# Moving the state sums of even chunks from GpSimd to VectorE, and one weighting of queries from VectorE to GpSimd

## The chip, the cores and the metric

The kernel runs on one core of one Trainium2 chip. The metric is the device time of one execution in microseconds. Engine names in the profile: PE is TensorE (PEld its weight loads), DVE is VectorE, ACT is ScalarE, POOL is GpSimd, SP is SyncE, which here only issues DMAs.

## The reference, cut to what matters

A gated linear attention over 4 batches, 8 heads, 768 positions and a head size of 48 feeds a mixture of eight experts. The change touches only the attention:

```python
state = zeros((B, H, D, D)); y = zeros_like(q)
for t in range(S):
    state = alpha[:, :, t, :, None] * state + einsum('bhd,bhe->bhde', k[:, :, t], v[:, :, t])
    y[:, :, t] = einsum('bhd,bhde->bhe', q[:, :, t], state)
```

The experts' part (a gate with argmax, `relu(x @ w1[e]) @ w2[e]` for each token's expert, times its gate) takes the last two thirds of the time and is the same in both kernels.

## The kernel before, in words

The 768 positions are cut into chunks of 128, 6 for each batch, so 24 chunks in all (`i` is 0 to 23; `i % 6` is the place within its batch). Even and odd chunk make a pair `p`. The loop at line 1060 goes over `UNITS`: rounds 0 and 1 take chunks 0 and 1 singly, rounds 2 to 11 the pairs (2,3) to (20,21), rounds 12 and 13 chunks 22 and 23 singly. All five queues are in manual order there: each engine runs its instructions in the order in which the Python program issues them.

Each round `n` works on three units at once:

- VectorE prepares unit `n`. `decay` (line 346) runs a backward scan over the decay factors (L349), takes the chunk's whole decay into `amin` (L352) and weights the keys (L357 to L359). `decay_back` (line 362) runs a scan forward (L365, L366) and weights the queries (L367). The scan L349 needs the pairwise products `pp` of `products` (L325), and L367 needs queries that `queries` (L332) has multiplied by alpha in place; GpSimd does both for a later pair, except that in round 2 VectorE does `queries` for its own pair (2,3).
- TensorE takes unit `n-1` through `natural` (transposes of the keys, L378, which ScalarE copies out as `knat`, L380), `update` (the key-value product of each chunk, L454), `scores` (L390; ScalarE copies them out, L394, GpSimd masks them, L395) and `state` (L416, queries times the carried state `T1`). `update` is not run for the last chunk of a batch.
- Units `n-2` (`outputs`, L428) and `n-3` (`rows`, L472, and `logits`, L491, every other round) follow.

In `update`, ScalarE copies the product from PSUM to the SBUF tile `S1` (L456), and GpSimd adds the carried state (L459, left out for the first chunk of a batch) and multiplies by the decay, which gives the state for the next chunk, `T1[(i + 1) % 4]` (L461). So `state` of chunk `i` needs the L461 of chunk `i - 1`; for the odd chunk of a pair that is the even chunk of the same unit, in the same round.

The order on TensorE in a round is: `natural` and `rows` (and `logits`), then `update`, `outputs(n-2)`, `scores` of the even chunk, `scores` of the odd chunk, `state`.

PSUM has eight banks. Two hold the decay factors `GF`, two the tile `y`, and the other four are one ring, in which `natural`, `rows`, `logits`, `update` and `scores` take the next place in turn (line 89: the names `tr`, `rt`, `lg` and `sc` are all `(lps, "tr", 4)`). A place is free again when the last reader of its old tile is done. `update` takes one place, and `scores` two for each chunk (line 385), so the second tile of the odd chunk's scores is the fourth tile after `update`'s and takes its place. Within `scores` the two tiles of a chunk are written by turns.

The program closes the loop's pools after round 13 and goes on with the experts, whose first weights and rows come by DMAs that the routing on VectorE sets off in rounds 12 and 13.

Of the kernel before, what the change touches and what calls it, by code (L numbers as in the profile page):

```python
# [16 lines left out]
ALU = mybir.AluOpType  # L17
# [7 lines left out]
B, H, S, D = 4, 8, 768, 48  # L25
# [48 lines left out]
def attention_moe(ctx: ExitStack, tc: tile.TileContext, q, k, v, alpha, mid, wg, mb, w1, w2, turned, rowsv, small, out):  # L74
    nc = tc.nc
    vec, act, pool, pe, sp = nc.vector, nc.scalar, nc.gpsimd, nc.tensor, nc.sync
# [41 lines left out]
    def turns(shape):  # L118
        return ring_tile("lg", shape)
# [13 lines left out]
    PP = [na.tile([W, 2 * NP * SG + 1], F32, name=f"pp{i}") for i in range(2)]  # L133
# [40 lines left out]
    def load_part(p, z, c0=0, c1=2):  # L174
        t = TAP[p % NA2] if z == 2 else TKP[z][p % NB]
        return sp.dma_start(t[:, c0 * KW : c1 * KW], turned[p, :, z * K2 + c0 * KW : z * K2 + c1 * KW])
# [46 lines left out]
    GF = GT[:, : 2 * NP * SG]  # L223
# [15 lines left out]
    T1 = []  # L239
# [76 lines left out]
    def span(u):  # L316
        return u[0] // 2, u[0] % 2 * NP, (u[-1] % 2 + 1) * NP

    def pairs(t, a, b):
        return t.rearrange("w (s m e) -> w s m e", m=HP, e=2)[:, a:b]  # L320
# [8 lines left out]
    def queries(u, by):  # L329
        p, a, b = span(u)  # L330
        x = pairs(TK[1][p % NB], a, b)
        by.tensor_tensor(x[:, :, :, 0], x[:, :, :, 0], pairs(TA[p % NA2], a, b)[:, :, :, 0], op=ALU.mult)  # L332

    def scaled(u, name):
        n = len(u)
        t = (na if n == 2 else sb).tile([W, n, NP, P], F32, name=f"{name}{n}", bufs=2)
        for c, i in enumerate(u):
            st[i, name] = t[:, c]
        return pairs(t.rearrange("w c a t -> w (c a t)"), 0, n * NP)

    def factors(a, b):
        f = GF.rearrange("w (s m) -> w s m", m=SG)[:, a:b, :HP].unsqueeze(3)
        f = f.broadcast_to([W, b - a, HP, 2])
        return bass.AP(f.tensor, f.offset, [*list(f.ap)[:-1], [1, 2]])
# [17 lines left out]
    def decay_back(u):  # L362
        p, a, b = span(u)
        x, y = a * SG, b * SG
        vec.reciprocal(GF[:, x:y:SG], GF[:, x:y:SG])  # L365
        scan = vec.tensor_tensor_scan(GF[:, x:y], PP[p % 2][:, x:y], GF[:, x:y], 0.0, op0=ALU.mult, op1=ALU.max)  # L366
        vec.tensor_tensor(scaled(u, "q"), pairs(TK[1][p % NB], a, b), factors(a, b), op=ALU.mult)  # L367
        return scan

    def guard(p):  # L370
        act.activation(
# [26 lines left out]
    def tiles4():  # L398
        for h in range(2):
            for g in range(2):  # L400
                for c in range(2):
                    yield 2 * h + c, h, g, slice(64 * c, 64 * c + 64)

    def place_of(i, g, h):
        return slice((i % 2 * 2 + h) * P, (i % 2 * 2 + h + 1) * P)

    def state(u):
        y = ps.tile([P, 2, 4 * P], F32, name="y")
        st[u, "new"] = {(g, c): True for g in range(2) for c in range(2)}
        for i in u:  # L410
            st[i, "Y"] = y
            if i % NC == 0:
                continue
            for j, h, g, z in tiles4():
                r = slice(64 * g, min(64 * g + 64, W))
                pe.matmul(  # L416
                    y[z, g, place_of(i, g, h)],
                    T1[i % 4][r, j],
                    st[i, "q"][r, j],
                    start=st[u, "new"].pop((g, j % 2), False),  # L420
                    stop=False,
                )

    def outputs(u):
# [17 lines left out]
        for i in u:  # L442
            st[i, "yt"] = yt

    def update(u):
        u = [i for i in u if i % NC < NC - 1]
        if not u:
            return
        kv = turns([W, len(u), NP, D])
        for c, i in enumerate(u):  # L450
            kn, vt = st[i, "n"], VT[i % NV]
            for h in range(H):
                r = slice(64 * (h % 2), min(64 * (h % 2) + 64, W))
                pe.matmul(kv[r, c, h // 2], kn[:, h // 2, r], vt[:, h * D : (h + 1) * D], start=True, stop=True)  # L454
        S1 = na.tile([W, 2, NP, D], F32, name="S", bufs=2)
        act.copy(S1[:, : len(u)], kv)  # L456
        for c, i in enumerate(u):
            if i % NC > 0:
                pool.tensor_tensor(S1[:, c], S1[:, c], T1[i % 4][:, :, :D], op=ALU.add)  # L459
            A = amin[:, i + 1].unsqueeze(2).broadcast_to([W, NP, D])  # L460
            pool.tensor_tensor(T1[(i + 1) % 4][:, :, :D], S1[:, c], A, op=ALU.mult)  # L461

    def rows(u):
        if u[0] < NF:
# [586 lines left out]
    def unit(n):  # L1051
        return UNITS[n] if 0 <= n < NN else ()
# [7 lines left out]
    for n, u in enumerate(UNITS):  # L1060
        p = u[0] // 2
        ahead = u[0] % 2 == 0
        if n == 0:
            load_part(2, 2)
        if n == 4:
            sp.dma_start(xd[MID : MID + 1], zr)
            sp.dma_start(gd[MID : MID + 1], zr[:, 0:1])
        if n == 0:
            products(u, vec)
            queries(u, pool)  # L1070
            products((1,), pool)
        if ahead and p + 1 < NPR and n > 3:
            products((2 * p + 2, 2 * p + 3), pool)
        scan = decay(u)
        if n == 2:
            queries(u, vec)
        last = u[-1] % 2 == 1
        done = [i for i in unit(n - 3) if i % LB == LB - 1]
        turned_now = [i for i in unit(n - 1) if i % NC < NC - 1]
        if not done:  # L1080
            for i in turned_now:
                natural(i)
        if n == 2:
            guard(0)
        if ahead and n and p + 2 < NPR:
            behind(load_part(p + 2, 2), scan)
        if last and p + 2 < NPR:
            load_part(p + 2, 0)
        if n <= 2:
            fill(2)  # L1090
        if unit(n - 3):
            rows(unit(n - 3))
        for i in done:
            logits(i, LB)
        if done:
            for i in turned_now:
                natural(i)
        for i in done:
            logits_rows(i, LB)
        spot()  # L1100
        if n == NN - 2:
            next(first_early)
        if n == NN - 1:
            for _ in first_early:
                pass
            run_later()
        scan = decay_back(u)
        if n == 0:
            queries((1,), pool)
        if ahead and n and p + 1 < NPR:  # L1110
            behind(load_rows(p + 1), scan)
        for i in done:
            if i == GROUPS[0][0]:
                logits_sum(i - LB, LB)
            if i >= GROUPS[0][0]:
                logits_sum(i, LB)
            groups(i)
            if i == GROUPS[1][0]:
                first_early = group_flow(*GROUPS[1][1:])
                next(first_early)  # L1120
                next(first_early)
            if i == GROUPS[2][0]:
                now["s"] += 1
                advance(2)
                second_half(st["chosen"])
        if last and p + 2 < NPR:
            load_part(p + 2, 1)
        if n == 6:
            vec.tensor_copy(prev_, rev)
        if n == 9:  # L1130
            half_index()
        if n == 1:
            bias = bias_table()
        update(unit(n - 1))
        if last and n > 2:
            guard(p)
        if n == 1:
            products((2 * p + 2, 2 * p + 3), pool)
        if n == NN - 2:
            next(first_early)  # L1140
            next(first_early)
        if unit(n - 3):
            rows_out(unit(n - 3))
        if unit(n - 2) and n != 2:
            outputs(unit(n - 2))
        for i in unit(n - 1):
            scores(i)
        if n == 2:
            outputs(unit(n - 2))
        if unit(n - 1):  # L1150
            state(unit(n - 1))
        if n in (2, 3):
            products((2 * p + 2, 2 * p + 3), pool)
        if last and 1 <= p and p + 1 < NPR and n > 1:
            queries((2 * p + 2, 2 * p + 3), pool)
        if n == 2:
            guard(p)
        if n == 1 or 4 <= n <= 6:
            next(bias, None)
        if 5 <= n <= 9:  # L1160
            next(consts, None)
        if n == 1:
            fill(2)
        spot()
        if NN - 3 <= n < NN - 1:
            next(first_early)
        if NN - 4 <= n < NN - 2:
            held_out((n - NN + 4) * NF // 2, NF // 2)
# [280 lines left out]
    op0 = layer2_sum(hs[0], w2s[0], 0, 2)  # L1449
# [6 lines left out]
    op1 = layer2_sum(hs[0], w2s[0], 1, 2)  # L1456
# [11 lines left out]
    for n in range(1, len(seq)):  # L1468
# [4 lines left out]
        x, w = n % NX, n % 2  # L1473
# [160 lines left out]
```

## Time and profile before

| what | value |
|---|---|
| time, median of 3 runs | 331.51 us (331.22 to 332.39) |
| time of the profiled execution | 332.0 us |
| its span, first to last instruction | 330.2 us |
| mean granted TensorE clock | 0.995 |
| busy in the span: PE, DVE, ACT, POOL | 315.9, 199.0, 190.2, 187.1 us |

The span is cut into 40 slices of 8.3 us on the profile's page; there TensorE stands at 9 tenths from the fourth to the last but one, VectorE in slices 2 to 9, and GpSimd in the fourth and in slices 6 to 10. The attention loop ends at about 106 us. The time of the profiled execution is 1.8 us more than its span.

### The profile page before, as it was taken

The numbers are of one execution on the slowest core, as the hardware profiler recorded it, in microseconds if no ns is written. First come the engines' busy times: TensorE is split into PE (matmuls) and PEld (weight loads), VectorE is DVE, ScalarE is ACT, GpSimd is POOL, SyncE is SP. The second block draws the span as 40 slices with busy tenths as digits, with TensorE's granted clock in tenths as the row PEclk, the third lists the DMA queues.
The fourth block names the chain that finished last, engine by engine and source line by source line (L and its number), as shares of the span: only waits on it lengthen the run. The fifth ranks groups of instructions, "written<-read, shape, count | busy, mean of one in ns | idle before, by whom it ended". The sixth has DMA issues, their size and how long they took to land.

```text
span 330.2 us, 8690 instructions
## 1 busy us (share of the span) xinstructions
PE 315.9 (96%) x3417; PEld 278.9 (84%) x3418; DVE 199.0 (60%) x380; ACT 190.2 (58%) x344; POOL 187.1 (57%) x259
## 2 busy tenths in 40 slices
PE   8889999999999999999999999999999999999992
PEld 3678888897987779999889988998899888888991
DVE  5999999997784668883671575157515660175200
ACT  3777878787866543565436743674367444664210
POOL 6779799999783540778886396239423801230121
PEclk9999999999999999999999999999999999999997
DMA  7988998999678497996586198419742673100011
GB/s 255 414 304 282 325 299 284 311 286 318 207 225 308 148 318 268 355 326 204 152 198 227 37 278 219 136 36 289 231 138 40 229 164 123 48 30 0 3 50 55
DMA packets 44038, 67.04 MB, mean 203 GB/s; under 512 B 15993, under 2 KB 30488, under 8 KB 43988
## 3 DMA queue, kind: packets, MB, share of 16 engines
q1 hardware_dynamic: 37652, 53.50, 51.9%
q0 software_dynamic: 4000, 9.68, 8.4%
q10 hardware_dynamic: 2336, 3.22, 2.7%
q8 instruction: 29, 0.48, 0.6%
q14 instruction: 21, 0.17, 0.2%
HBM read 53.79 MB, written 9.50 MB: 192 GB/s over the span
## 4 chain that ended last, share of the span: by engine, by line
PE 61%; POOL 15%; issue 12%; DVE 6%; DMA 3%; ACT 2%; POOLq 1%; ACTq 0%; DVEq 0%
PE sc L1331 8%; PE sc L1333 8%; PE sc L1332 8%; PE tr L1352 7%; PE tr L1351 7%; PE tr L1350 7%; POOL scT L395 4%; PE tr L165 3%; PE y L428 3%; POOL pp L325 3%; POOL tq L332 2%; PE tr L390 2%; PE tr L472 2%; POOL S L459 2%; POOL out_dram L1272 2%
## 5 line engine op out<-in xcount | busy, mean ns | idle before, releaser
L1272 POOL DMA_INDIRECT out_dram<-os,odx x23 | 23.5, 1021 | 84.7 <-ACT os L1365 78.4
L1331 PE MATMUL sc<-w2H,hH 128*128 128x384 f32 x192 | 64.8, 338 | 0.0
L1333 PE MATMUL sc<-w2H,hL 128*128 128x384 f32 x192 | 64.3, 335 | 0.0
L1332 PE MATMUL sc<-w2L,hH 128*128 128x384 f32 x192 | 64.2, 334 | 0.0
L1015 ACT ACTIVATE hH<-tr 128x512 fp32r<-128x512 f32 x47 | 28.1, 598 | 49.0 <-PE tr L1352 43.0
L1350 PE MATMUL tr<-xH,w1H 128*128 128x512 f32 (+1 forms) x144 | 53.9, 374 | 0.0
L1352 PE MATMUL tr<-xH,w1L 128*128 128x512 f32 (+1 forms) x144 | 53.5, 372 | 0.0
L1351 PE MATMUL tr<-xL,w1H 128*128 128x512 f32 (+1 forms) x144 | 53.5, 372 | 0.0
L1017 DVE SCALAR_TENSOR_TENSOR hL<-tr,hH 128x512 fp32r<-128x512 f32 x47 | 32.3, 689 | 29.8 <-ACT hH L1015 29.6
L885 POOL DMA_INDIRECT xg<-xd,idx x25 | 27.4, 1097 | 19.9 <-DVE vals L671 13.0
L1365 ACT ACTIVATE os<-sc,gg 128x384 f32<-128x384 f32 x23 | 13.4, 582 | 43.1 <-PE sc L1333 41.5
L1323 DVE TENSOR_TENSOR xL<-xg,xH 128x512 fp32r<-128x512 f32 x12 | 8.3, 692 | 48.5 <-ACT xH L1322 48.5
L1331 PEld LDWEIGHTS sc<-w2H,hH 128*128 128x128 f32 x192 | 36.0, 188 | 1.2 <-issue 1.0
L1332 PEld LDWEIGHTS sc<-w2L,hH 128*128 128x128 f32 x192 | 36.1, 188 | 0.2
L1333 PEld LDWEIGHTS sc<-w2H,hL 128*128 128x128 f32 x192 | 36.0, 188 | 0.1
L891 POOL DMA_INDIRECT gg<-gd,idx x25 | 27.3, 1092 | 11.0 <-issue 7.0
L395 POOL TENSOR_SCALAR_AFFINE_SELECT scT<-scT 128x512 f32<-128x512 f32 x48 | 28.9, 635 | 7.8 <-ACT scT L394 7.8
L1352 PEld LDWEIGHTS tr<-xH,w1L 128*128 128x128 f32 x144 | 27.1, 188 | 5.0 <-DVE w1L L1035 0.5
L1351 PEld LDWEIGHTS tr<-xL,w1H 128*128 128x128 f32 x144 | 27.1, 188 | 4.7
L1350 PEld LDWEIGHTS tr<-xH,w1H 128*128 128x128 f32 x144 | 27.1, 188 | 4.5
L1035 DVE TENSOR_TENSOR w1L<-w1r,w1H 128x768 fp32r<-128x768 f32 x24 | 23.0, 997 | 8.8 <-ACT w1H L1033 8.6
L1035 DVE TENSOR_TENSOR w2L<-w2r,w2H 128x768 fp32r<-128x768 f32 x24 | 26.4, 1100 | 0.7
(280 smaller groups left out, 608.0 us busy)
## 6 DMA issues: line engine op xcount, KB each, us to landing
w1r<-in_moe_w_dram SPq DMA_DIRECT2D x16, 768.0 KB, 7.8
w2r<-in_moe_w_dram SPq DMA_DIRECT2D x16, 768.0 KB, 6.5
ta<-in_turned_dram SPq DMA_DIRECT2D x11, 512.0 KB, 4.9
tk<-in_turned_dram SPq DMA_DIRECT2D x11, 512.0 KB, 5.1
tq<-in_turned_dram SPq DMA_DIRECT2D x11, 512.0 KB, 6.4
vt<-in_rowsv_dram SPq DMA_DIRECT2D x11, 384.0 KB, 4.7
xd<-xs ACTq DMA_DIRECT2D x7, 384.0 KB, 6.3
xd<-w2r SPq DMA_DIRECT2D x2, 768.0 KB
```

Of the source, the lines that this page charges most:

```text
L395: pool.affine_select(s, s, [[0, NP], [1, P]], ALU.is_ge, 0.0, base=0, channel_multiplier=-1)
L885: pool.indirect_dma_start(xg[x][:, u], None, xd[0:rows], IOA(idx[:, c : c + 1], 0), bounds_check=rows - 1, oob_is_err=False)
L1015: act.activation(hH, hp, AF.Relu)
L1017: vec.scalar_tensor_tensor(hL, hp, 0.0, hH.bitcast(F32), op0=ALU.max, op1=ALU.subtract)
L1035: vec.tensor_tensor(lw, src, hi.bitcast(F32), op=ALU.subtract)
L1272: return pool.indirect_dma_start(to, IOA(odx[:, c : c + 1], 0), t, None, bounds_check=N - 1, oob_is_err=False)
L1331: pe.matmul(op, hH[:, us] if f is None else hH[:, f, us], wH, start=first, stop=False)
L1332: pe.matmul(op, hH[:, us] if f is None else hH[:, f, us], wL, start=False, stop=False)
L1333: pe.matmul(op, hL[:, us] if f is None else hL[:, f, us], wH, start=False, stop=final)
L1350: pe.matmul(hp, wH[:, d, fs], XH[:, d, :n], start=(d == 0), stop=False)
L1351: pe.matmul(hp, wH[:, d, fs], XL[:, d, :n], start=False, stop=False)
L1352: pe.matmul(hp, wL[:, d, fs], XH[:, d, :n], start=False, stop=(d == ND - 1))
```

## The change

`queries` for pair (2,3) moves from VectorE in round 2 to GpSimd in round 1, behind that round's `state`. `decay_back` is split behind its scan: from round 4 on, `update` of unit `n-1` is called between the scan (L366) and the weighting of the queries (L367, now `decay_queries`), where it stood behind both and behind the routing work of the round before. In `update`, for units that begin with chunk 4 or a later even chunk, the even chunk's add and multiply go to VectorE, which adds in place in PSUM (`kv[:, 0]`) and writes `T1` from there; ScalarE copies only the odd chunk to `S1`, and nothing where the odd chunk ends a batch. The odd chunk's add and multiply stay on GpSimd.

```diff
     def decay_back(u):
         p, a, b = span(u)
         x, y = a * SG, b * SG
         vec.reciprocal(GF[:, x:y:SG], GF[:, x:y:SG])
-        scan = vec.tensor_tensor_scan(GF[:, x:y], PP[p % 2][:, x:y], GF[:, x:y], 0.0, op0=ALU.mult, op1=ALU.max)
+        return vec.tensor_tensor_scan(GF[:, x:y], PP[p % 2][:, x:y], GF[:, x:y], 0.0, op0=ALU.mult, op1=ALU.max)
+
+    def decay_queries(u):
+        p, a, b = span(u)
         vec.tensor_tensor(scaled(u, "q"), pairs(TK[1][p % NB], a, b), factors(a, b), op=ALU.mult)
-        return scan
...
+    BY_VEC = 4
+
     def update(u):
...
+        c0 = 1 if u[0] >= BY_VEC and u[0] % 2 == 0 else 0
         S1 = na.tile([W, 2, NP, D], F32, name="S", bufs=2)
-        act.copy(S1[:, : len(u)], kv)
+        if len(u) > c0:
+            act.copy(S1[:, c0 : len(u)], kv[:, c0:])
         for c, i in enumerate(u):
+            by, s = (vec, kv[:, c]) if c < c0 else (pool, S1[:, c])
             if i % NC > 0:
-                pool.tensor_tensor(S1[:, c], S1[:, c], T1[i % 4][:, :, :D], op=ALU.add)
+                by.tensor_tensor(s, s, T1[i % 4][:, :, :D], op=ALU.add)
             A = amin[:, i + 1].unsqueeze(2).broadcast_to([W, NP, D])
-            pool.tensor_tensor(T1[(i + 1) % 4][:, :, :D], S1[:, c], A, op=ALU.mult)
+            by.tensor_tensor(T1[(i + 1) % 4][:, :, :D], s, A, op=ALU.mult)
...
         scan = decay(u)
-        if n == 2:
-            queries(u, vec)
...
         scan = decay_back(u)
+        if n > 3:
+            update(unit(n - 1))
+        decay_queries(u)
...
-        update(unit(n - 1))
+        if n <= 3:
+            update(unit(n - 1))
...
             state(unit(n - 1))
+        if n == 1:
+            queries((2 * p + 2, 2 * p + 3), pool)
```

## Rows read from the trace of the kernel before

**Rows 1.** The page's first part: busy time, share of the span, instructions.

```profile
PE 315.9 (96%) x3417; PEld 278.9 (84%) x3418; DVE 199.0 (60%) x380; ACT 190.2 (58%) x344; POOL 187.1 (57%) x259
```

**Rows 2.** The chain that ended last: start us, us, what.

```profile
38.90 2.40 POOL scT L395 x4
...
77.56 0.52 POOL T L461
```

**Rows 3.** Busy time in one stretch: length, then each engine, clock, DMA.

```profile
58.00:78.00 20.00, 19.49 (x479) 17.62 (x474) 17.56 (x29) 16.82 (x33) 19.20 (x29) 1.00 0.92 294
```

**Rows 4.** Waits of PEld and of DVE, 24 to 106 us: total, times, longest.

```profile
PEld tr L454 <- ACT knat L380: 3.6, 10, 0.7
PEld y L416 <- POOL T L461: 1.1, 2, 0.7
...
DVE rk L601 <- ACT kept L115: 4.8, 2, 3.4
```

**Rows 5.** VectorE in order of time, rounds 2 to 4: start, us, what.

```profile
15.88 1.57 DVE L332 TENSOR_TENSOR tq<-tq,ta 112x512 f32<-112x512 f32 x1
...
20.20 1.25 DVE L349 TENSOR_TENSOR_SCAN GF<-pp,GF 112x520 f32<-112x520 f32 x1
...
26.53 1.25 DVE L349 TENSOR_TENSOR_SCAN GF<-pp,GF 112x520 f32<-112x520 f32 x1
...
30.19 1.25 DVE L366 TENSOR_TENSOR_SCAN GF<-pp,GF 112x520 f32<-112x520 f32 x1
```

**Rows 6.** GpSimd in order of time.

```profile
18.98 1.51 POOL L332 TENSOR_TENSOR tq<-tq,ta 112x512 f32<-112x512 f32 x1 [2.08 <-DMA tq<-in_turned_dram]
...
25.19 1.04 POOL L325 TENSOR_TENSOR pp<-ta 112x512 f32<-112x512 f32 x1
...
29.34 0.51 POOL L461 TENSOR_TENSOR T<-S,amin 112x192 f32<-112x192 f32 x1
...
43.96 1.04 POOL L325 TENSOR_TENSOR pp<-ta 112x512 f32<-112x512 f32 x1
```

**Rows 7.** The load of pair (2,3)'s queries on SP, and such loads' landing times.

```profile
6.58 0.48 SPq L176 DMA_DIRECT2D tq<-in_turned_dram  x1
...
DMA to landing us min/median/max: 4.7/6.1/7.4
```

**Rows 8.** TensorE in order of time.

```profile
27.34 1.98 PE L390 MATMUL tr<-q,k 48*64 48x128 f32 x64
29.14 1.42 PE L416 MATMUL y<-q,T 64*64 64x128 f32 x32
...
50.11 0.61 PE L454 MATMUL tr<-vt,knat 128*64 128x48 f32 x15 [0.50 <-ACT knat L380]
...
75.20 1.98 PE L390 MATMUL tr<-q,k 48*64 48x128 f32 x64
...
78.12 0.67 PE L416 MATMUL y<-q,T 64*64 64x128 f32 x16 [0.51 <-POOL T L461]
```

**Rows 9.** GpSimd's adds, and two VectorE operations of other sizes.

```profile
L459 POOL TENSOR_TENSOR S<-S,T 112x192 f32<-112x192 f32 x9 | 5.4, 595 | 0.3
...
L359 DVE TENSOR_TENSOR k<-tk,GF 112x512 f32<-112x512 f32 x8 | 5.5, 690 | 0.3
...
120.28 0.26 DVE L773 TENSOR_TENSOR nj<-kv,thr 128x96 f32<-128x96 f32 x1 [0.52 <-PE kv L772]
```

**Rows 10.** VectorE in order of time, the first scans of rounds 7 and 10.

```profile
46.12 1.25 DVE L349 TENSOR_TENSOR_SCAN GF<-pp,GF 112x520 f32<-112x520 f32 x1
...
69.46 1.23 DVE L349 TENSOR_TENSOR_SCAN GF<-pp,GF 112x520 f32<-112x520 f32 x1
```

**Rows 11.** The end: TensorE's last matmul, then busy time and clock by stretch.

```profile
323.37 0.34 PE L1333 MATMUL sc<-w2H,hL 128*128 128x384 f32 x1
...
326.00:327.00 1.00, 0.00 (x0) 0.00 (x0) 0.00 (x0) 0.00 (x0) 0.00 (x0) 0.87 0.57 201
327.00:328.00 1.00, 0.00 (x0) 0.00 (x0) 0.00 (x0) 0.00 (x0) 0.00 (x0) 0.50 0.07 20
```

## The prediction

> **What bounds the kernel now.** I read the page first. By busy time TensorE fills 96% of the span [rows 1], which says little of a stage, so I went to the chain of waits. From 38.9 to 78 us it runs almost only through GpSimd: masks, products, query weightings, state sums, one behind the other, until the state multiply that ends at 78.08 [rows 2]. A reader who stops there would say that GpSimd bounds the loop. But busy time by stretch shows TensorE busy for 19.49 of 20 us between 58 and 78, as much as GpSimd's 19.20, and VectorE at 17.56 [rows 3]. And TensorE's waits from round 4 to the loop's end show what GpSimd costs it: 1.1 us for the state multiply, in two places. The larger one, 3.6 us for `knat`, is a trip from TensorE to ScalarE and back, which the change leaves alone [rows 4]. So GpSimd's 39 us in the chain hide about 1 us of loss; TensorE's own work lies right below. I then read VectorE, GpSimd and TensorE in order of time, to place the moved instructions between their neighbours.
>
> **The change part by part.**
>
> *Queries of pair (2,3).* VectorE loses one instruction of 1.57 us at 15.88 [rows 5]; the next one follows some 1.5 us after its start, so round 2 ends, with a little lost between dependent operations, 1.3 us earlier, and the first scan of round 3 starts at 18.9 instead of 20.2 [rows 5]. GpSimd must do it in time. Its load is issued at 6.58 and lands within 7.4 us, by 14.0 at the latest [rows 7]; the weighting then runs to 15.5 at a price of 1.51 [rows 6]. That pushes round 2's work on GpSimd back by up to 2 us, but GpSimd stands for 2.08 us ahead of 18.98, waiting for the next pair's queries [rows 6], and this wait hides it; without it the 1.5 us would stay on GpSimd's queue. What is late next is the product for round 4's scan: it lies behind that same DMA on GpSimd and ends at 26.23 [rows 6]. VectorE, free by 25.1, waits for it, and round 4 starts at 26.3 instead of 26.53 [rows 5]. Of 1.3 us VectorE keeps 0.2; TensorE keeps more, since its scores in round 4 can start up to 1.2 us before their 27.34 [rows 8] (their queries come from round 3).
>
> *Price of a sum on VectorE.* No row has 192 elements with a source in PSUM. Below lies 0.26 us for 96 elements out of PSUM, above it 0.69 for 512 [rows 9]; on a line between them 192 elements take 0.36. GpSimd's 0.60 for the same add [rows 9] is the far end. I take 0.35, so 0.8 for an add and a multiply that depend on each other, and 0.4 for a multiply alone.
>
> *Where the sum stands.* This decides. In round 4 GpSimd did the multiply for chunk 4 at 29.34 to 29.85 [rows 6], and TensorE's `state` waited for it a little. Now it stands on VectorE behind round 4's forward scan. That scan starts 3.66 us after the round's first (30.19 less 26.53 [rows 5]), so at 29.96; it ends at 31.2, and add and multiply at 32.0: 2.2 us later than on GpSimd, though each is cheaper.
>
> *What waits for it.* `state` of chunk 5, and before it something that the diff doesn't name. The even chunk's product now stays in its PSUM place until VectorE's multiply is done; ScalarE's copy used to free it right behind the product. The ring has four places, and the fourth tile after it is the second one of chunk 5's scores. On TensorE round 4 then goes: scores of chunk 4 from 26.15 to 27.1 (half of the 1.8 us between 27.34 and 29.14 [rows 8]), a standstill to 32.0, scores of chunk 5 to 32.95, `state` to 33.95. Before, `state` ended at 29.14 + 1.42 = 30.56 [rows 8]. TensorE leaves round 4 later by 3.4 us. Queued behind are the rest of the loop and the experts; ScalarE's copies and GpSimd's masks of chunk 5's scores follow it.
>
> The standstill itself can have a price. The granted clock is 1.00 between 58 and 78 us [rows 3]. At the end TensorE's last matmul ends at 323.71; the clock averages 0.87 in the stretch 326 to 327 and 0.50 in the next [rows 11], so it fell from 2.4 to 1.2 GHz some 3 us after TensorE had stopped. A standstill of 4.9 us is longer than that; TensorE's longest wait from round 4 on was 0.7 [rows 4]. The Trainium skill (TensorE: Matmul & The Clock Gate, What's actually happening) calls the slow clock the resting state, which activity lifts; by that rule TensorE would come out of the standstill slow, and the trace's end agrees (0.50). I leave it out of the sum and take it as a rival.
>
> *Does it stay?* From round 5 on TensorE has its 3.4 us of lateness and hardly a wait to lose them in: only the one for GpSimd in round 10, 0.7 us on the weight loads [rows 4], 0.51 on the matmuls ahead of 78.12 [rows 8], goes, as GpSimd has less to do. VectorE is hardly late at first (its sum of 0.8 less the 0.2 that it gained), but then falls back. Round 7's product on GpSimd (43.96 [rows 6]) follows masks that are now 3.4 late, so its scan starts at 48.4 instead of 46.12 [rows 10]. In round 7 VectorE must wait for the key-value product (50.11 + 0.6 + 3.4 = 54.1 [rows 8]; its scan is done at 53.3), the new wait, with the queries' weighting and the routing behind it. With that 0.8 and 0.65, 0.3 and 0.65 us for rounds 7, 8 and 9 (0.8 or 0.4 of sums, less the short gap ahead of L367 that they fill), less one wait of 0.2, round 10 starts at 69.46 [rows 10] + 4.5 = 74.0. Its sum is done 5.7 us later (30.19 + 1.25 - 26.53 [rows 5], and 0.8), at 79.7. TensorE wants the ring's place at 75.20 + 3.4 + 0.95 = 79.55 [rows 8], so the two meet there at almost no cost. In round 10 `state` ends at 81.5 instead of 78.8: 2.7 us late. In rounds 12 and 13 VectorE had waited 4.8 us for ScalarE's copies of the routing counts [rows 4]; they cover its lateness, and the first expert's loads keep theirs within about 0.4 us of TensorE's. ScalarE's copies that go were off the path. The experts then start 2.7 us late and end so.
>
> **Sum.** 332.0 us for the profiled execution, + 3.4 - 0.7 = 334.7. It lies 0.5 above the median of 331.5, so I predict **334.2 us**.
>
> **The rivals.**
>
> *The place is not what stops TensorE; only `state` is.* If the second scores tile finds another place, chunk 5's scores finish by 28 and only its `state` waits until 32.05 and ends at 32.6: 2.0 later, less the 0.7, so 1.3 and 332.8. For it: the trace of before shows no wait on this place. Against it: the names of the ring all lead to one pool of four.
>
> *The clock falls in the standstill.* Against it speaks that no pause inside the loop did that, for it that none was so long. No row has TensorE working at 1.2 GHz. If that lasts as long as the clock took to fall at the end, 3 us, it loses half of it, 1.5: 335.7. I keep up to twice this (337.2). A VectorE price near GpSimd's 0.60 ends there too: 13 sums in rounds 4 to 11 at 0.25 more are 3.3 us, most of them on VectorE's own chain.
>
> *Faster: VectorE's sums come in time.* Place: round 4. If chunk 4's sum were done before TensorE reaches the scores of chunk 5 (27.1), or the first `state` that needs it (28.5), there is no standstill; that is the point from which it decides. TensorE then keeps the 1.2 us from round 3 and its two waits for GpSimd, 1.1 us [rows 4], 2.3 at most; VectorE's 13 sums would take about half of that back in rounds 8 to 11. 1.2 faster: 330.3. For it: the chain on GpSimd [rows 2], out of which some 7 us go. Against it: VectorE would need to be 3.5 us earlier than round 4's product on GpSimd allows.
>
> *No change.* The gains of the last case against a wait of some 1.5 us: about 331.5.
>
> **How the numbers follow.** Forecast (334.2) 0.46; only `state` waits (332.8) 0.12; the clock, or dearer sums (335.7) 0.20; no change 0.10; faster 0.12. A measurement can tell 0.3%, about 1 us, from no change, so faster is 0.12, same 0.10, slower 0.78. The range runs from 331.4, in the middle of the no-change case, to 337.0, near the clock case's far end: outside lie the faster case, half of no change, and a few hundredths above.
>
> **What would show it.** Right: in round 4 a wait of 4 to 5 us on TensorE in L390, released by VectorE's multiply; the first scan of round 4 at 26.3, behind GpSimd's product; VectorE's sums at 0.35 us; `state` in round 4 ending about 3.4 later than at 30.56, and the last matmul about 2.7 later. If the wait is in L416, the first rival is right; if the clock is below 1.00 behind it, the second. Wrong: no wait on TensorE over 1 us in round 4, or a lateness that shrinks before 100 us, which would say that TensorE had slack that I didn't see.

## The result, and the profile after

The changed kernel takes 336.79 us (median of four executions, 335.76 to 338.22) against 331.5 (331.22 to 332.39): a ratio of 1.0146, interval 1.0107 to 1.0186. It is slower by 5.3 us by the medians, by 4.8 by the ratio. The profiled execution takes 336.09 us, 4.1 more than the 332.0 of before; the prediction was +2.7.

The first part of the page of the changed kernel, and from its second part the granted clock by slices:

```profile
span 334.4 us, 8668 instructions
...
PE 316.9 (95%) x3417; PEld 280.4 (84%) x3418; DVE 201.4 (60%) x396; ACT 187.7 (56%) x340; POOL 179.3 (54%) x243
...
PEclk9999899999999999999999999999999999999999
```

GpSimd has 7.8 us less to do than in [rows 1], VectorE only 2.4 us more, and the span is 4.2 us longer. So the busy times, read alone, say the opposite of the result. Only the clock shows a mark: an 8 in the fifth slice, 33 to 42 us.

The waits of TensorE's matmuls, 24 to 112 us (total, times, longest):

```profile
PE tr L392 <- DVE T L469: 4.5, 1, 4.5
PE tr L459 <- ACT knat L382: 1.2, 3, 0.5
PE tr L480 <- ACT kept L115: 0.3, 1, 0.3
```

One wait of 4.5 us is new, on the scores (L392, L390 before) and released by VectorE's multiply; the waits for GpSimd's multiply in [rows 4] are gone. In order of time TensorE shows it so (start, us, what, idle time before it):

```profile
26.37 1.30 PE L392 MATMUL tr<-q,k 48*64 48x128 f32 x34
32.17 1.47 PE L392 MATMUL tr<-q,k 48*64 48x128 f32 x27 [4.50 <-DVE T L469]
...
33.44 2.11 PE L418 MATMUL y<-q,T 64*64 64x128 f32 x31
...
35.71 1.19 PE L480 MATMUL tr<-ident,yt 128*128 128x128 f32 x8
...
76.57 1.04 PE L480 MATMUL tr<-ident,yt 128*128 128x128 f32 x8
...
79.90 1.98 PE L392 MATMUL tr<-q,k 48*64 48x128 f32 x64
81.70 1.05 PE L418 MATMUL y<-q,T 64*64 64x128 f32 x32
82.68 1.09 PE L480 MATMUL tr<-ident,yt 128*128 128x128 f32 x8
...
327.35 0.34 PE L1345 MATMUL sc<-w2H,hL 128*128 128x384 f32 x1
```

The transposes L480 are a good gauge of lateness, since they open a round; the same rows of before (there L472) are

```profile
30.66 1.09 PE L472 MATMUL tr<-ident,yt 128*128 128x128 f32 x8
...
71.88 1.04 PE L472 MATMUL tr<-ident,yt 128*128 128x128 f32 x8
78.72 1.09 PE L472 MATMUL tr<-ident,yt 128*128 128x128 f32 x8
```

So TensorE is 5.05 us late behind round 4, 4.69 in round 10 and 3.96 in round 11; the last matmul is 327.35 - 323.37 [rows 11] = 3.98 late. Everything is lost in one place. VectorE there:

```profile
26.47 1.25 DVE L349 TENSOR_TENSOR_SCAN GF<-pp,GF 112x520 f32<-112x520 f32 x1 [1.02 <-POOL pp L325]
...
30.14 1.25 DVE L366 TENSOR_TENSOR_SCAN GF<-pp,GF 112x520 f32<-112x520 f32 x1
31.29 0.34 DVE L467 TENSOR_TENSOR tr<-tr,T 112x192 f32<-112x192 f32 x1
31.66 0.36 DVE L469 TENSOR_TENSOR T<-tr,amin 112x192 f32<-112x192 f32 x1
```

VectorE is early enough to wait 1.02 us for GpSimd's product, goes through round 4's whole weighting, and only then adds and multiplies. The multiply ends at 32.02 and TensorE goes on at 32.17.

The last part of the loss stands in the clock. Stretches of round 4 (length, then busy time of PE, PEld, DVE, ACT, POOL, granted clock, DMA share, GB/s):

```profile
31.00:32.00 1.00, 0.00 (x0) 0.00 (x0) 0.96 (x4) 0.00 (x0) 0.00 (x0) 1.00 0.75 164
32.00:33.00 1.00, 0.83 (x22) 0.86 (x26) 1.00 (x2) 0.00 (x0) 0.00 (x0) 0.77 0.77 305
33.00:34.00 1.00, 1.00 (x26) 1.00 (x24) 0.90 (x2) 0.07 (x1) 0.00 (x0) 0.50 0.57 182
34.00:35.00 1.00, 1.00 (x26) 1.00 (x21) 0.97 (x3) 1.00 (x2) 0.42 (x1) 0.50 0.90 280
35.00:36.00 1.00, 1.00 (x13) 0.62 (x7) 0.97 (x3) 0.18 (x1) 1.00 (x3) 0.53 0.94 299
36.00:37.00 1.00, 1.00 (x16) 0.83 (x18) 0.93 (x3) 0.51 (x2) 1.00 (x1) 1.00 0.90 299
```

TensorE stopped at 27.67; the clock is 0.50 (1.2 GHz) from about 32.5 to 35.9, so it fell just as work came back. From 32.17 to the row at 35.71 are 3.54 us. The same work, the odd chunk's half of the scores and `state`, takes 1.95 us in experiment 9 below, where nothing stops it. So 1.6 us are the clock's, and 5.05 - 1.6 = 3.45 the standstill's. The clock row says the same: from 32.54 to 35.71 TensorE ran at half speed, and half of that is 1.6.

### The profile page after: what moved, and what is told of

It reads as the page before. It is cut to its first block, busy times and chain, and to the rows that moved or that the text cites. A ratio compares the mean times of both kernels' runs of the same rounds, so it can differ in the third digit from the quotient of the medians.

```text
span 334.4 us, 8668 instructions
## 1 busy us (share of the span) xinstructions
PE 316.9 (95%) x3417; PEld 280.4 (84%) x3418; DVE 201.4 (60%) x396; ACT 187.7 (56%) x340; POOL 179.3 (54%) x243
## 4 chain that ended last, share of the span: by engine, by line
PE 73%; issue 11%; POOL 4%; DMA 3%; ACT 3%; DVE 2%; POOLq 1%; SPq 1%; ACTq 0%
PE sc L1343 8%; PE sc L1345 8%; PE sc L1344 7%; PE tr L1364 7%; PE tr L1362 7%; PE tr L1363 7%; PE tr L392 6%; PE y L430 5%; PE tr L480 3%; PE tr L459 3%; PE tr L165 3%; PE y L418 2%; PE tr L380 2%; POOL out_dram L1284 2%; DMA vt<-in_rowsv_dram 2%
## 5 line engine op out<-in xcount | busy, mean ns | idle before, releaser
L1335 DVE TENSOR_TENSOR xL<-xg,xH 128x512 fp32r<-128x512 f32 x12 | 8.3, 692 | 48.4 <-ACT xH L1334 48.4
L392 PE MATMUL tr<-q,k 48*64 48x128 f32 x736 | 24.1, 277 | 4.5 <-DVE T L469 4.5
```

The lines of the kernel that those rows point to most:

```text
L392: pe.matmul(pp[g][z, j], kh[r, j, z], qh[r, j], start=True, stop=True)
```

## The experiments

Three groups; each group ran on one chip beside the kernel before, so ratios are compared, not times. On the chip of the second group each of the four profiled kernels had a stand of 2.6 to 2.8 us on ScalarE, near 100 us, without a releaser in the program; in experiments 5, 6 and 7 the granted clock was at 0.50 for 3.4 us behind it. The kernel before was slower there too (336.52 us), and the intervals are wide.

| | what | ratio to before | interval |
|---|---|---|---|
| - | the change | 1.0146 | 1.0107 to 1.0186 |
| 1 | sums on VectorE from chunk 6 | 0.9989 | 0.9967 to 1.0011 |
| 2 | the queries' move alone | 0.9999 | 0.9976 to 1.0022 |
| 3 | product's place freed early | 1.0211 | 1.0181 to 1.0241 |
| 4 | TensorE kept busy in the standstill | 1.0066 | 1.0044 to 1.0088 |
| 5 | chunk 4's sum alone on VectorE | 1.0209 | 1.0169 to 1.0249 |
| 6 | the change again | 1.0175 | 1.0134 to 1.0217 |
| 7, 10 | GpSimd sums first | 1.0004, 0.9948 | 0.9966 to 1.0042, 0.9921 to 0.9975 |
| 8, 9 | the sum in VectorE's gap | 0.9979, 0.9941 | 0.9948 to 1.0009, 0.9915 to 0.9967 |

**1. Sums on VectorE from chunk 6.**

```diff
-    BY_VEC = 4
+    BY_VEC = 6
```

> The changed kernel with BY_VEC = 6: chunk 4's sum goes back to GpSimd, nine of the other sums in rounds 5 to 13 and the moved queries stay as changed. Theory A (the loss is made in round 4, by VectorE's sum for chunk 4 coming late): TensorE has no wait over 1 us there, and the time is that of the kernel before within 0.3%, 331.0 to 332.5 us, for VectorE's sums of the later rounds are done before TensorE asks for them. Theory B (VectorE's added work, some 0.6 us in each two-sum round, bounds the loop): most of the loss stays, 334.5 us or more, and VectorE's first scan of round 12 is 3 us or more later than 84.80.

Measured: no loss, and no gain either. VectorE does all its sums but chunk 4's, so neither its load nor its prices made the change slow. What is left in round 4 is a wait for GpSimd, 1.38 us where at most 1 was expected, since TensorE now comes earlier with its scores; in TensorE's order of time:

```profile
28.00 0.62 PE L418 MATMUL y<-q,T 64*64 64x128 f32 x16
30.00 0.67 PE L418 MATMUL y<-q,T 64*64 64x128 f32 x16 [1.38 <-POOL T L469]
...
30.77 1.82 PE L480 MATMUL tr<-ident,yt 128*128 128x128 f32 x8
```

The transposes at 30.77 take 1.82 instead of 1.09 us: here too the clock was at 0.50, from about 31.0 to 34.4, behind a wait of only 1.38. So this execution pays for the clock without the long standstill. That profiled execution took 333.08 us, at the upper end of this kernel's 330.99 to 333.17.

**2. The queries' move alone.**

```diff
-        if n == 2:
-            queries(u, vec)
...
+        if n == 1:
+            queries((2 * p + 2, 2 * p + 3), pool)
```

> The kernel before with only the first part of the change: queries of pair (2,3) on GpSimd in round 1. Theory A (GpSimd's product for round 4's scan takes back what VectorE gains): VectorE starts round 3 1.0 to 1.3 us earlier and round 4 at most 0.2 us earlier; TensorE's scores of round 4 start about 1 us earlier and its state then waits for GpSimd's multiply as before, so the time is 331.5 within 0.5 us. Theory B (VectorE's first rounds bound the loop's start): 1.3 us faster, 330.2 us.

Measured: no difference, and the clock stays at 1.00. VectorE waits for the product in round 4, and TensorE, early with the scores, waits for GpSimd in `state`:

```profile
26.65 1.25 DVE L349 TENSOR_TENSOR_SCAN GF<-pp,GF 112x520 f32<-112x520 f32 x1 [1.01 <-POOL pp L325]
```

```profile
30.27 0.67 PE L416 MATMUL y<-q,T 64*64 64x128 f32 x16 [1.31 <-POOL T L461]
```

The 1.3 us that VectorE gains run into GpSimd's queue on both sides.

**3. Free the place early.** ScalarE copies both chunks' products to SBUF, and VectorE adds there.

```diff
-        if len(u) > c0:
-            act.copy(S1[:, c0 : len(u)], kv[:, c0:])
+        act.copy(S1[:, : len(u)], kv)
...
-            by, s = (vec, kv[:, c]) if c < c0 else (pool, S1[:, c])
+            by, s = (vec if c < c0 else pool), S1[:, c]
```

> The changed kernel, but ScalarE copies both chunks' products to S1 as before, and VectorE adds and multiplies even chunks' sums there, in SBUF: the PSUM place is free right behind the product, chunk 4's state still comes from VectorE at about 32 us. Theory A (TensorE waited for the place): in round 4 the scores of chunk 5 run through, TensorE stops in state instead, from about 28.3 to 32.0, and leaves the round 1.4 us earlier than in the changed kernel; 335.4 us if the clock falls as there, 333.5 if it does not fall in the shorter standstill. Theory B (only the wait for the state counted, the place would have been free): no difference to the changed kernel, 336.8 us.

Measured: 339.68 us against 332.53, slower still. The time is a miss, the mechanism is not: the scores run through (x64), so the place was what had stopped them, and TensorE stops at the next thing that needs the sum, `state`:

```profile
27.03 1.98 PE L392 MATMUL tr<-q,k 48*64 48x128 f32 x64
28.83 0.62 PE L418 MATMUL y<-q,T 64*64 64x128 f32 x16
34.12 1.12 PE L418 MATMUL y<-q,T 64*64 64x128 f32 x16 [4.67 <-DVE T L468]
```

It stops as long as before, because the sum comes later. VectorE's add, and GpSimd beside it:

```profile
32.03 1.64 DVE L466 TENSOR_TENSOR S<-S,T 112x192 f32<-112x192 f32 x1
33.70 0.36 DVE L468 TENSOR_TENSOR T<-S,amin 112x192 f32<-112x192 f32 x1
```

```profile
31.97 1.48 POOL L332 TENSOR_TENSOR tq<-tq,ta 112x512 f32<-112x512 f32 x1
```

The add takes 1.64 us with both sources in SBUF, against 0.34 with one in PSUM; it began 0.06 behind GpSimd's weighting and ended 0.2 behind it, while the multiply after it took 0.36 with GpSimd done. The Trainium skill (SBUF — State Buffer, Who interferes with whom) says that a VectorE instruction with two SBUF inputs contends with a GpSimd instruction that reads SBUF; the trace agrees (1.64 beside GpSimd, 0.34 as the least without it). The product for round 4's scan comes 0.75 later, too. And the kernel pays once more behind round 4: `state` has a second wait for T, of 1.65 us ahead of 84.84, and the clock is at 0.50 twice, from about 34.2 to 37.6 and from 85.4 to 88.8, with TensorE at work in nearly all of it.

**4. Keep TensorE busy.** The changed kernel, with 18 matmuls of zeros added between the scores of chunks 4 and 5; they write a tile that nobody reads.

```diff
+            if i == 5:
+                keep = ps.tile([P, 4 * P], F32, name="y")
+                for _ in range(18):
+                    pe.matmul(keep, still[:, :P], still, start=True, stop=True)
```

> The changed kernel with 18 matmuls of zeros (128x512 bf16, into the free y tile, about 0.215 us each) between the scores of chunks 4 and 5, where TensorE stood still: they fill some 3.9 of the 4.9 us and change no result. Theory A (1.3 us or more of the loss are the slow clock behind the standstill): the granted clock stays at 1.00 through round 5, scores of chunk 5 and state take 1.9 us instead of 3.4, and the time is 334.2 to 334.6 us, with less spread between executions than the 2.5 us of the changed kernel. Theory B (the clock is beside the point, the whole loss is waiting): 336.8 us as the changed kernel.

Measured: 1.0066, about half of the loss is back. The zeros last until VectorE is done (its multiply ends at 31.83), and what follows runs at full clock:

```profile
27.34 4.04 PE L1160 MATMUL y<-xg 128*128 128x512 bf16 x18
31.32 1.55 PE L392 MATMUL tr<-q,k 48*64 48x128 f32 x29
...
32.72 1.13 PE L418 MATMUL y<-q,T 64*64 64x128 f32 x31
...
33.95 1.09 PE L480 MATMUL tr<-ident,yt 128*128 128x128 f32 x8
```

```profile
33.00:34.00 1.00, 1.00 (x32) 0.79 (x24) 0.95 (x1) 0.93 (x2) 0.27 (x1) 1.00 0.74 165
```

The row L480 is 3.29 late instead of 5.05 (up to 0.2 of that because VectorE's multiply ended earlier). The clock's share is 1.0146 - 1.0066 = 0.8% or 2.7 us; put together from the two intervals it lies between about 1.2 and 4.1. The spread between executions, which was expected to shrink, hardly did: 2.1 us against 2.5. The wait keeps 0.66%, 2.2 us. This profiled execution hides the gain at its end (it is the slowest of nine, 336.26 against a median of 334.8): it loses 1.2 us near 73 us, around a stand of 0.7 on TensorE that has no releaser.

**5 and 6. Chunk 4's sum alone on VectorE, and the change again beside it.**

```diff
-        c0 = 1 if u[0] >= BY_VEC and u[0] % 2 == 0 else 0
+        c0 = 1 if u[0] == BY_VEC else 0
```

> The changed kernel with one sum of the ten on VectorE, that of chunk 4; the other even chunks' sums are GpSimd's as before. Theory A (all of the loss is made in round 4): TensorE's wait of 4.5 us in the scores of chunk 5 is there, the clock falls behind it, and the time is that of the changed kernel within 0.5 us. Theory B (the later sums on VectorE add to the loss, by their work and the waits in front of them): 1 us or more faster than the changed kernel.

> The changed kernel itself, once more, beside the others of this call. Theory A: 1.0146 of the kernel before, within its interval (1.011 to 1.019), and several executions that differ by 1 to 2.5 us with the granted clock, since the slow stretch behind the standstill lasts differently long. Theory B (the spread of the first four executions was the chip's): as close together as the kernel before.

Measured: 1.0209 and 1.0175, which can't be told apart. One sum of the ten chunks carries the whole loss. The repeated kernel also shows that the clock's price changes from one execution to the next. The standstill is the same, the clock is not:

```profile
32.23 1.76 PE L392 MATMUL tr<-q,k 48*64 48x128 f32 x27 [4.50 <-DVE T L469]
```

```profile
30.00:31.00 1.00, 0.00 (x0) 0.00 (x0) 0.97 (x2) 0.00 (x0) 0.14 (x1) 0.96 0.87 352
31.00:32.00 1.00, 0.00 (x0) 0.00 (x0) 0.97 (x3) 0.00 (x0) 0.00 (x0) 0.50 0.78 147
...
36.00:37.00 1.00, 1.00 (x6) 0.95 (x7) 0.93 (x3) 0.18 (x1) 1.00 (x2) 0.50 0.98 307
37.00:38.00 1.00, 1.00 (x9) 0.75 (x11) 1.00 (x1) 0.48 (x2) 0.94 (x2) 0.63 0.82 291
```

Here it is at 0.50 from 30.9 to 37.7, 6.8 us instead of 3.4. TensorE works in 5.5 of them, at half speed, and so loses 2.75; with chunk 4 alone the same (0.50 from 30.7 to 37.5). That is close to the 2.7 that experiment 4 gives, though it is one execution of each kernel, and on another chip.

**7 and 10. GpSimd sums first.** VectorE gets only chunk 16's sum (round 10). In round 4 GpSimd does chunk 4's sum ahead of the queries and products for a later pair.

```diff
-    BY_VEC = 4
+    BY_VEC = 16
...
+        if n == 4:
+            queries(u, pool)
+            products((2 * p + 2, 2 * p + 3), pool)
```

The two calls stand behind `update`; the calls for this pair at the old places go, and `c0` is 1 for chunk 16 alone.

> Sums stay on GpSimd but for chunk 16's, which VectorE does in PSUM behind round 10's scan; and in round 4 GpSimd does chunk 4's sum first and the weighting of pair (6,7) and the product of pair (8,9) behind it. Theory A (in round 4 it is the place of the sum that counts, whichever engine does it): no wait of TensorE in round 4 over 0.5 us, which it then leaves about 1.5 us earlier than before, and none for GpSimd in round 10; GpSimd's queue takes back some 0.3 us in rounds 6 to 8; 0.8 to 1.5 us faster than the kernel before, ratio 0.996. Theory B (TensorE has no slack to gain, or GpSimd's queue holds it from round 5 on): ratio 0.999 to 1.001.

> The kernel with GpSimd's sum first once more, for the same reason. Theory A: TensorE leaves round 4 at about 29.3 instead of 30.6 and keeps 0.8 to 1.2 us of it to the end; ratio 0.996 to 0.998. Theory B: the gain is taken back; ratio 0.999 to 1.001.

Measured: 1.0004 on the second group's chip, which decides nothing, and 0.9948 on the third's: faster by 0.5%. GpSimd's order in the second run:

```profile
26.57 0.59 POOL L467 TENSOR_TENSOR S<-S,T 112x192 f32<-112x192 f32 x1
27.24 0.51 POOL L469 TENSOR_TENSOR T<-S,amin 112x192 f32<-112x192 f32 x1
27.71 1.53 POOL L332 TENSOR_TENSOR tq<-tq,ta 112x512 f32<-112x512 f32 x1
```

The sum is done at 27.75 by the slower engine, 2.1 us earlier than in [rows 6] and 4.3 earlier than VectorE had it.

**8 and 9. The sum in VectorE's gap.** The 1 us in which VectorE waits for GpSimd's product at the start of round 4 is used for chunk 4's sum, so TensorE must do `natural`, `rows` and `update` first (their calls at the old places go for this round); chunk 16's sum stays where the change put it; the others go back to GpSimd (`c0` is 1 for the chunks in `BY_VEC`).

```diff
-    BY_VEC = 4
+    BY_VEC = (4, 16)
...
+        if n == 4:
+            natural(4)
+            rows(unit(1))
+            update(unit(3))
         scan = decay(u)
```

> VectorE does chunk 4's sum as in the changed kernel, in PSUM, but ahead of round 4's first scan, where it stood for 1 us waiting for GpSimd's product (the keys' transposes, the rows and the key-value product of that round go ahead of the scan in program order, which changes no order on TensorE but that of the product against VectorE); besides, chunk 16's sum in round 10, and GpSimd keeps the others. Theory A (place, not engine): the same instruction that cost 5 us costs nothing; VectorE's round 4 starts within 0.3 us of the changed kernel's, TensorE has no wait over 0.5 us in round 4 and the kernel is 1.0 to 2.0 us faster than the one before, ratio 0.995. Theory B (a sum on VectorE holds the PSUM place or the scan too long wherever it stands): slower than the kernel before.

> The kernel of the sum in the gap once more, because in the last call TensorE and VectorE stood for 2 to 3 us at places where the profile shows no releaser of the kernel, in all four kernels. Theory A (place, not engine): without those stands TensorE keeps the 1.5 us by which it left round 4 earlier, less 0.2 to 0.5 in rounds 5 to 11; ratio to the kernel before 0.995 to 0.997. Theory B (the gain is taken back behind the loop, where the first expert waits for its weights or rows): ratio 0.999 to 1.001.

Measured: 0.9979 on the second group's chip, which is not clear of no change, and 0.9941 on the third's, 330.77 us against 332.79: faster than the kernel before. It can't be told apart from experiment 10 (0.9948), so in time either engine gives the same. VectorE in round 4 of the second run, then TensorE:

```profile
25.24 0.36 DVE L467 TENSOR_TENSOR tr<-tr,T 112x192 f32<-112x192 f32 x1
25.63 0.36 DVE L469 TENSOR_TENSOR T<-tr,amin 112x192 f32<-112x192 f32 x1
26.33 1.25 DVE L349 TENSOR_TENSOR_SCAN GF<-pp,GF 112x520 f32<-112x520 f32 x1 [0.34 <-POOL pp L325]
```

```profile
26.24 1.98 PE L392 MATMUL tr<-q,k 48*64 48x128 f32 x64
28.03 1.05 PE L418 MATMUL y<-q,T 64*64 64x128 f32 x32
...
29.18 1.09 PE L480 MATMUL tr<-ident,yt 128*128 128x128 f32 x8
```

The same two instructions of VectorE on the same PSUM tile, 6 us earlier, and the scan behind them starts no later (26.33 against 26.47). TensorE is now 30.66 - 29.18 = 1.5 us ahead of the kernel before, and its last matmul (321.90) is 1.47 ahead of [rows 11].

## Why the prediction was right, and where its size was off

*The standstill* was right in place, cause and size: a wait of 4 to 5 us in L390 (now L392), released by VectorE's multiply, because the product holds the ring's place. Predicted end 32.0, measured 32.17; predicted loss 3.4, measured 3.45. Experiment 3 shows that the place stops the scores (without it they run through), which rules out the rival in which only `state` waits; experiments 1 and 5 show that nothing else in the change costs time that can be measured.

*What made the sum late* was right: round 4's scan at 26.3 behind GpSimd's product (26.47), the sum behind the second scan, add and multiply at 0.35 each (0.34 and 0.36).

*The queries' move*: it ends at GpSimd's product and GpSimd's multiply, as costed, and is worth nothing (experiment 2).

*The step that was mis-sized is the clock.* The prediction wrote that the standstill can have a price, and left it out of the sum as a rival of 1.5 us. It measured 1.6 in the profiled execution, 2.75 in the repeated one and 2.7 between the medians, within the 3 that the rival kept as its far end. The argument against it, that no pause inside the loop had lowered the clock, was empty, as the prediction itself said that none was as long; the only row of before with a comparable pause, the end [rows 11], shows the fall. The likeliest case should have been the clock's, 335.7, with the 336.8 measured nearer to it. The forecast of 334.2 is 2.6 below the median, as much as the clock takes. That the median fell inside the range is in part luck: it lies 0.2 below the upper end of 337.0, and experiment 6's ratio would put it at 337.3. The Trainium skill's rule that the prediction cited (TensorE: Matmul & The Clock Gate, What's actually happening), by which the slow clock is the resting state and activity lifts it, agrees with the traces: 0.50 out of each of the four stops of 4.5 us or more (the change, experiments 3, 5 and 6), and 1.00 again with TensorE at work.

*Does it stay?* Yes. The 0.7 that comes back in round 10 was predicted and measured (4.69 late in round 10, 3.96 in round 11), with 0.36 more in rounds 5 to 10, which was not predicted. The sum: 3.45 + 1.6 - 0.36 - 0.73 = 3.96 us, against 3.98 at the last matmul and 4.1 in the execution's time.

*VectorE in the later rounds* was later than worked out: round 7's first scan at 49.89 instead of 48.4, the sum of round 10 done at 80.18 instead of 79.7. One wait was not foreseen, VectorE's in round 5:

```profile
40.60 0.36 DVE L469 TENSOR_TENSOR T<-tr,amin 112x192 f32<-112x192 f32 x1 [2.44 <-ACT S L463]
```

Its last releaser is ScalarE's copy of the other chunk out of the same tile, but the key-value product itself was done only at 40.19, some 0.4 us earlier. So it is above all a wait for TensorE, which came 5 us late out of round 4; the prediction expected such a wait first in round 7, where it was 0.94 us. A second one like it, 1.16 us, comes in round 11. They cost TensorE nothing: no wait of TensorE's above is for them, nor does its lateness grow in rounds 5 to 10.

*The rival on the other side*, sums in time, fell with the standstill; experiments 8 and 9 reach its point by another order of instructions. They gain about what it was given, 1.2 us (experiment 9: 1.5 in the trace, 2.0 between the medians; experiment 8: not clear of nothing).

**Left open.** Why the low clock lasts 3.4 us in some executions and 6.8 in others, why it fell behind a wait of 1.38 us in experiment 1 and not behind one of 1.31 in experiment 2, and the stands without a releaser. What the clock costs the change is known only as 1.6 to 2.75 us by the traces and 1.2 to 4.1 by the times. In experiment 9 the shares of the earlier scores and of round 10's wait weren't measured apart.

## What to carry to other kernels

Moving work to a cheaper, less busy engine pays only if it arrives there before its old place; in a queue in fixed order the start is set by what stands ahead of it, and 0.7 us of sums behind 4.8 us of scans and weightings cost 5 us. Arriving in time is not enough either: the nine sums that did so gained nothing in experiment 1, where TensorE had hardly a wait for them to remove. Ask also what the late instruction still holds: here a place of a PSUM ring, which stopped TensorE one stage before the consumer that the diff names. And when a forecast contains a stop of TensorE of several microseconds, put the slow clock behind it into the sum, not among the rivals.

## What the runs showed of the hardware

- The clock fell in or just behind all four stops of TensorE of 4.5 to 4.7 us (the change, experiments 3, 5 and 6), and behind shorter ones of 1.38 us (experiment 1) and 1.65 (experiment 3). It did not fall behind one of 1.31 (experiment 2), nor behind one of 2.01 (experiment 8).
- It was low for 3.4 or 6.8 us, and the cost was 1.6 to 2.75 us for one and the same 4.5 us stop.
- 4 us of matmuls of zeros in the gap kept it at 1.00 (experiment 4).
- A VectorE add of 112 x 192 took 0.34 us with a source in PSUM and 1.64 with both in SBUF beside GpSimd (experiment 3).
